# The transposed mixing matrix on the sync queue: half pieces, one a segment, and where its read-back is issued

## The chip, the cores and the metric

The kernel runs on one core of one Trainium2 chip. The metric is device time in microseconds (us), the median of several runs of one program. One further execution is taken by the hardware profiler; the rows in this document are from such profiles.

The engines are named as in the profile: PE is the matrix engine (PEld its weight loads), ACT, DVE and POOL the three elementwise engines, SP the engine that here issues nearly all DMAs. The 16 DMA engines move the data. Each engine works through its own list in order; an instruction waits for the semaphores that it needs, and what stands behind it in the list waits too.

## The reference

A block of attention with a recurrent memory, and then a gated MLP that mixes along the sequence. S = 2048 tokens, width 512, 32 heads of 128, segments of 32 tokens, 8 memory rows, MLP half width 896. Cut to what matters:

```python
mem = mem0
for s in range(64):                                  # part A
    h = concat([mem, ln(x)[32*s:32*s+32]])           # 40 rows
    q, k, v = h @ Wq, h @ Wk, h @ Wv                 # 32 heads
    o = softmax(mask(q @ k.T * scale)) @ v
    o = o @ Wo
    mem, out[s] = o[:8], o[8:]
h = x + concat(out)
z = gelu(ln(h) @ w_in)                               # part B
z1, z2 = z[..., :896], ln(z[..., 896:])
g = w_sp @ z2 + b_sp[:, None]                        # w_sp: 2048 x 2048
h2 = h + (z1 * g) @ w_out
```

The memory rows of a segment come out of the segment before, so the 64 segments of part A run one after the other.

## The kernel before

**Part A** is a loop over `s` (L945 to L1113) that emits one segment after the other. The order in which the code adds operations is the order in which each engine executes them; waits follow from what each operation reads and writes, and from `after=`, a list of operations to wait for. In a segment PE runs, in this order:

- Q and K of 32 rows (L495, 512 columns, four column groups side by side), with the memory rows of the segment before put in by small matmuls (L680);
- scores (L554, L560), the value rows (L495), softmax sums (L575, L496);
- one batch group of matmuls for later segments (L414, L433 or L775);
- probabilities times values (L623, L629), the output projection of eight memory-free rows of earlier segments (L707);
- output sums (`Wo`, L495 and L496 with `f_cT`). They come in two halves by output column: columns 0 to 255 into bank `OB`, evacuated by ACT (`part_evac`, L671), then columns 256 to 511 into `OB2`, evacuated by DVE (L673). The memory rows of the next segment follow from both.

Q, K and V of the last eight rows of each segment don't depend on the memory. They are computed in batches of 16 segments ("batched" rows). The batched V rows go to DRAM (`vext_d`, store L455) and come back segment by segment into one of three buffers `Vx` (`load_vx`, L477), which L629 reads.

**What SP issues for part B beside part A.** The matmul of part B needs `w_sp` transposed. It is read from DRAM in 32 pieces of 64 rows by a transposing DMA into `wst` (L809) and written to DRAM scratch `wT_d` (L810):

```python
def wT_piece(i):
    sp(lambda e: e.dma_start_transpose(out=wst[:, :, :], in_=B_w_sp[i * 64:(i + 1) * 64, :]), writes=["wst"])
    sp(lambda e: e.dma_start(wT_d[i], wst[:, :, :]), reads=["wst"], writes=[("wTd", i)])
```

A piece is issued at the head of each odd segment. There is one buffer `wst`, and the write waits on SP until the transpose has landed. The other DMAs of the loop: `load_h` (L701) and `load_x` (L290) at the head of every fourth segment; the stores of finished rows `h_d` (L728, at the end of segments with s % 4 = 3), `xn_d` (L736, s % 4 = 1), of batch groups (`vext_d` L455, `z2p_d` L786); from segment 36 on the loads of `w_in` (L766) and transposes of `xn_d` (L747). `load_vx(s + 2)` stands near the end of segment s, behind the batch group's store and ahead of the store of `xn_d`.

**Part B** begins in the last segment. `z2_back` (L937) reads rows of z2 from DRAM, `load_wT(0)` (L933) reads the first quarter of the transposed matrix (eight pieces of 256 KB) over the Q weights, behind the last Q matmul (`lastop["q"]`). In the program it stands after the loop, behind four `z2_back` loads and all stores of segment 63, and nine more `z2_back` loads follow. ACT applies the activation to z2 (L1207), DVE normalises it (L1158 to L1169), and PE multiplies it with the transposed matrix (`mix`, L1183), with z1 groups (L1176) between.

Of the kernel before, what the change touches and what calls it, by code (L numbers as in the profile page):

```python
# [169 lines left out]
def fast_path(nc, st, keep, A_x, A_mem0, A_Wq, A_Wk, A_Wv, A_Wo, A_seg_len, B_w_in, B_w_sp, B_b_sp, B_w_out, out):  # L170
# [7 lines left out]
    NSEG = S // SEG  # L178
# [16 lines left out]
    em = Emitter(n_dma_sems=40)  # L195

    def sb(name, shape, dt):
        return st.enter_context(nc.sbuf_tensor("f_" + name, shape, dt))
# [5 lines left out]
    def region(off, n):  # L204
        return arena[:, off:off + n]
# [26 lines left out]
    wst = sb("wst", [128, RB, 64], BF)  # L232
# [25 lines left out]
    wT_d = nc.dram_tensor("wT_d", [S // 64, 128, RB, 64], BF, kind="Internal").ap()  # L258
# [7 lines left out]
    def PB(b):  # L266
        return ("ps", b)

    def sp(fn, **k):
        return em.add("sp", fn, dma=True, **k)  # L270

    def pe(fn, **k):
        return em.add("pe", fn, **k)

    def act(fn, **k):
        return em.add("act", fn, **k)

    def dve(fn, **k):
        return em.add("dve", fn, **k)
# [194 lines left out]
    def load_vx(s):  # L474
        i = s % CK
        assert all(("vext", s // CK, n) in em.last_w for n in range(8))
        sp(lambda e: e.dma_start(Vx[:, s % NVX, :, :], vext_d[s // CK, 8 * i:8 * i + 8, :, :, :].rearrange("t b g e -> g t b e")),  # L477
           reads=[("vext", s // CK, n) for n in range(8)], writes=[("Vx", s % NVX)])
# [14 lines left out]
    def tile_mm(e, out, lhsT, rhs, start, stop, c, held=False):  # L493
        if not held:
            return e.matmul(out, lhsT=lhsT, rhs=rhs, start=start, stop=stop, skip_group_check=True, tile_position=(0, 32 * c))  # L495
        return e.add_instruction(mybir.InstMatmult(  # L496
            name=nc.get_next_instruction_name(), ins=[e.lower_ap(rhs), e.lower_ap(lhsT)], outs=[e.lower_ap(out)],
            start_tensor_calc=start, stop_tensor_calc=stop, tile_size=(128, 32), tile_position=(0, 32 * c),
            bass_skip_group_check=True, ldweights=False))
# [89 lines left out]
    def sm_rcp(b):  # L589
        act(lambda e: e.activation(out=R_sb[:, b, :], in_=R_sb[:, b, :], func=ACT.Exp, scale=-1.0, bias=RBIAS),  # L590
            reads=[("R", b)], writes=[("R", b)])
# [58 lines left out]
    def Wo(cs, bank, d0, d1, bs=(0, 1), first=(0, 0), last=(3, 1), held=None):  # L650
        for c in cs:
            for bg in (4 * b + g for b in bs for g in range(4)):
                b, g = bg // 4, bg % 4
                h = 16 * b + 4 * c + g
                i = 8 * c + bg
                pe(lambda e, h=h, g=g, i=i, b=b, c=c: tile_mm(
                    e, ps[32 * g:32 * g + 32, bank, 0:d1 - d0], cTh[:, i, 8:40], w_o[:, h, d0:d1], (c, b) == first,
                    (c, b) == last, g, (c, b) == held),
                    reads=[("cT", c), ("Wo", b, c)], writes=[PB(bank)])
# [7 lines left out]
    def part_evac(s, half):  # L667
        bank, d0 = (OB, OB2)[half], OC * half
        dst, src = part[:, s % 8, d0:d0 + OC], ps[:, bank, 0:OC]
        if half == 0:  # L670
            act(lambda e: e.activation(out=dst, in_=src, func=ACT.Copy), reads=[PB(bank)], writes=[("part", s % 8, 0)])  # L671
        else:
            dve(lambda e: e.tensor_copy(out=dst, in_=src), reads=[PB(bank)], writes=[("part", s % 8, 1)])  # L673

    def mem_out(s, half):
        bank = GB[half]
        for dc in range(2 * half, 2 * half + 2):
            for c in range(4):
                c0 = dc * 128 + 32 * c
                pe(lambda e, dc=dc, c=c, c0=c0: e.matmul(ps[32 * c:32 * c + 32, bank, dc * M:(dc + 1) * M], lhsT=part[:, s % 8, c0:c0 + 32],  # L680
                                                         rhs=G_sb[:, :], start=True, stop=True, skip_group_check=True, tile_position=(0, 32 * c)),
                   reads=[("part", s % 8, half), "G"], writes=[PB(bank)])
        d2 = slice(2 * half, 2 * half + 2)
        src = ps[:, bank, 2 * half * M:(2 * half + 2) * M].rearrange("p (dc c) -> p dc c", c=M)
        act(lambda e: e.activation(out=hT[:, slot(s + 1), d2, 0:M], in_=src, func=ACT.Copy),  # L685
            reads=[PB(bank)], writes=[("hTm", s + 1, half)])
# [13 lines left out]
    def load_h(rb):  # L700
        sp(lambda e: e.dma_start(hbuf[:, rb % 2, :], xr[:, rb, :]), writes=[("h", rb % 2)])  # L701
# [44 lines left out]
    def xn2T_dma(rb, after):  # L746
        sp(lambda e: e.dma_start_transpose(out=xT2(rb), in_=xn2_d[rb]), reads=[("xn2d", rb)], writes=[("xn2T", rb)],  # L747
           after=after)
# [4 lines left out]
    def xT2(rb):  # L753
        return xts[rb // 4][:, rb % 4, :, :]
# [8 lines left out]
    def load_w_in(half, dc, after):  # L763
        t = (w_in1[:, dc, :], w_in2[dc])[half]
        tok = ("w_in1", "w_in2")[half]
        sp(lambda e: e.dma_start(t, winr[:, dc, half * FH:(half + 1) * FH]), writes=[(tok, dc)], after=after)  # L766
        em.mark_const((tok, dc))
# [37 lines left out]

    NWT = S // 64

    def wT_piece(i):
        sp(lambda e: e.dma_start_transpose(out=wst[:, :, :], in_=B_w_sp[i * 64:(i + 1) * 64, :]), writes=["wst"])  # L809
        sp(lambda e: e.dma_start(wT_d[i], wst[:, :, :]), reads=["wst"], writes=[("wTd", i)])  # L810


    act(lambda e: e.preload_act_table_set("natural_log_exp_and_others"))
# [18 lines left out]
    def start_x(ck, i):  # L832
        start_group(qkx_mm, qkx_evac, ck, i)
# [83 lines left out]
    for ck, n0 in ((2, 2), (3, 0)):  # L917
        for n in range(n0, 8):
# [3 lines left out]
    wTb = [region(0, RB * 512).rearrange("p (t sc c) -> p t sc c", sc=RB, c=64),  # L922
           region(3 * WSZ, RB * 512).rearrange("p (t sc c) -> p t sc c", sc=RB, c=64)]
# [4 lines left out]
    gt = region(2 * WSZ + RB * FH, 2048).bitcast(F32).rearrange("p (j t) -> p j t", j=2)  # L928
    w_out = region(3 * WSZ + RB * 512, FB * D).rearrange("p (fb d) -> p fb d", fb=FB)

    def load_wT(tb, after):
        for t in range(8):
            sp(lambda e, t=t: e.dma_start(wTb[tb % 2][:, t, :, :], wT_d[8 * tb + t]), reads=[("wTd", 8 * tb + t)],  # L933
               writes=[("wT", tb % 2, t)], after=after)

    def z2_back(r0, r1, after):
        sp(lambda e: e.dma_start(z2[:, r0:r1, :], z2p_d[r0:r1].rearrange("r p f -> p r f")),  # L937
           reads=[("z2p", r, hf) for r in range(r0, r1) for hf in range(2)],
           writes=[("z2", r, hf) for r in range(r0, r1) for hf in range(2)], after=[after])

    lastop = {}
# [3 lines left out]
    for s in range(NSEG):  # L945
        j4 = s % 4
        rb = s // 4
        if j4 == 0 and rb > 0:
            load_h(rb - 1)
        if s == NSEG - 1:  # L950
            load_h(rb)
        if s % 2 == 1 and s < NSEG - 1:
            wT_piece(s // 2)
        if s == NSEG - 2:
            wT_piece(NWT - 1)
        if j4 == 0 and 2 <= rb + 2 < RB:
            load_x(rb + 2, 0)
        if s == 4:
# [39 lines left out]
        sm_ln(1)  # L998
        sm_rcp(1)
        if s == NSEG - 1:  # L1000
            xn2T_dma(8, [xops[s]])
            for r in range(4):
                z2_back(r, r + 1, lastop["v"])
        if s + 1 < NSEG:
            qx_copy(s + 1)
# [39 lines left out]
        if s == 0:  # L1045
            start_x(1, 9)
            Wo((0, 2, 1), OB, 0, OC)
            Wo((0, 2, 1), OB2, OC, D)
            Wo((3,), OB, 0, OC)
            part_evac(s, 0)  # L1050
            Wo((3,), OB2, OC, D)
            part_evac(s, 1)
            late += gv.pour(2)
            mem_out(s, 0)
            late += gv.pour(2)
        else:
            Wo((0, 2, 1, 3), OB, 0, OC)
            part_evac(s, 0)
            Wo((3,), OB2, OC, D, (1, 0), (3, 1), (1, 1), (3, 1))
            Wo((0, 2), OB2, OC, D, (0, 1), (3, 1), (1, 1))  # L1060
            if s + 1 < NSEG:
                mem_out(s, 0)
            Wo((1,), OB2, OC, D, (0, 1), (3, 1), (1, 1))
            part_evac(s, 1)
# [22 lines left out]
            late.append(lambda: ring_copy(rb + 2, XB))  # L1087
        for f in late:
            f()
        if s + 2 < NSEG:  # L1090
            load_vx(s + 2)
        if j4 == 1 and rb >= 2:
            xn2_apply(rb - 2, rb % 2)
            xn2_store(rb - 2, rb % 2)
# [7 lines left out]
        if c2 + 8 <= s < c3:  # L1102
            k, m = (s - c2 - 8) // 2, s % 2
# [3 lines left out]
        if s in (c3 + 2, c3 + 4, c3 + 6, c3 + 10, c3 + 14):  # L1107
            r = 9 + (c3 + 2, c3 + 4, c3 + 6, c3 + 10, c3 + 14).index(s)
            xn2T_dma(r, [sops[c3 + 2 * (r - 9) + 1]])
        if s in (c3 + 5, c3 + 7, c3 + 11, c3 + 13):  # L1110
            dc = (c3 + 5, c3 + 7, c3 + 11, c3 + 13).index(s)
            load_w_in(0, dc, [xops[c3 + (3, 6, 10, 13)[dc]]])
    load_wT(0, [lastop["q"]])  # L1113
    for r in range(4, NP):
        z2_back(r, r + 1, lastop["v"])
    sp(lambda e: e.dma_start(bsp_b, bass.AP(B_b_sp.tensor, B_b_sp.offset, [[0, 128], [1, S]])), writes=["bsp"], after=[lastop["k"]])
# [138 lines left out]
    endA = em.by_eng["pe"][-1]  # L1255
    WoX_evac(RB - 1)
    load_wT(1, [endA])
    sp(lambda e: e.dma_start(w_out, B_w_out.rearrange("(fb p) d -> p fb d", p=128)), writes=["w_out"], after=[endA])
    xn2T_pe(RB - 2, 0)
# [755 lines left out]
def build_kernel(nc, A_x, A_mem0, A_Wq, A_Wk, A_Wv, A_Wo, A_seg_len, B_x, B_w_in, B_w_sp, B_b_sp, B_w_out, out):  # L2015
    args = (A_x, A_mem0, A_Wq, A_Wk, A_Wv, A_Wo, A_seg_len, B_w_in, B_w_sp, B_b_sp, B_w_out, out)
    with contextlib.ExitStack() as keep:
        with contextlib.ExitStack() as st:
            em, sems, dsems, flag = fast_path(nc, st, keep, *args)
# [88 lines left out]
```

## Time and profile before

| | us |
|---|---|
| median of three timed runs (854.01 to 854.50) | 854.24 |
| the profiled execution, its own time | 853.86 |
| its span, first to last instruction | 851.7 |
| PE busy in the span | 837.0 |
| DVE, ACT, POOL busy | 538.8, 427.1, 159.8 |

A row of a group gives line, engine, operation, tiles written and read, count, then busy time and mean; in brackets or behind a bar stands the idle time ahead of it and what ended it. "issue" is idle time in which the engine waited for nothing that the profile shows. In the view of stretches, each row is one stretch of time with each engine's busy time and its count of instructions. [...]

### The profile page before, as it was taken

The numbers are of one execution on the slowest core, as the hardware profiler recorded it, in microseconds if no ns is written. First come the engines' busy times: TensorE is split into PE (matmuls) and PEld (weight loads), VectorE is DVE, ScalarE is ACT, GpSimd is POOL, SyncE is SP. The second block draws the span as 40 slices with busy tenths as digits, with TensorE's granted clock in tenths as the row PEclk, the third lists the DMA queues.
The fourth block names the chain that finished last, engine by engine and source line by source line (L and its number), as shares of the span: only waits on it lengthen the run. The fifth ranks groups of instructions, "written<-read, shape, count | busy, mean of one in ns | idle before, by whom it ended". The sixth has DMA issues, their size and how long they took to land.

```text
span 851.7 us, 43893 instructions
## 1 busy us (share of the span) xinstructions
PE 837.0 (98%) x20921; PEld 447.0 (52%) x19133; DVE 538.8 (63%) x1256; ACT 427.1 (50%) x1151; POOL 159.8 (19%) x404
## 2 busy tenths in 40 slices
PE   6999999999999999999999999999999999999997
PEld 5754445555555555556555555555554544444443
DVE  3456677676666666676766666767666676553443
ACT  2455565656555655555655555565656566500000
POOL 5111121122121112121212121211112123200000
PEclk9999999999999999999999999999999999999999
DMA  9972322223212122121323222233322369032001
GB/s 319 379 227 59 75 56 57 54 47 82 57 34 75 34 65 62 26 72 47 64 58 85 55 74 51 81 70 85 91 57 80 96 184 366 2 112 105 33 12 40
DMA packets 105614, 77.21 MB, mean 91 GB/s; under 512 B 63304, under 2 KB 90960, under 8 KB 105424
## 3 DMA queue, kind: packets, MB, share of 16 engines
q1 hardware_dynamic: 105424, 74.35, 30.3%
q8 instruction: 159, 2.61, 1.3%
q14 instruction: 31, 0.25, 0.1%
HBM read 42.38 MB, written 21.59 MB: 75 GB/s over the span
## 4 chain that ended last, share of the span: by engine, by line
PE 95%; DMA 2%; SPq 1%; issue 0%; ACT 0%; DVE 0%; POOL 0%; POOLq 0%
PE f_ps L495 46%; PE f_ps L1183 11%; PE f_ps L496 8%; PE f_ps L414 6%; PE f_ps L707 4%; PE f_ps L1300 3%; PE f_ps L623 3%; PE f_ps L1176 2%; PE f_ps L433 2%; PE f_ps L775 2%; PE f_ps L554 1%; PE f_ps L575 1%; DMA f_arena<-in_A_Wk_dram 1%; PE f_ps L629 1%; PE f_ps L439 1%; PE f_ps L680 1%
## 5 line engine op out<-in xcount | busy, mean ns | idle before, releaser
L495 PE MATMUL f_ps<-f_arena,f_hT 128*32 128x512 bf16 x5120 | 359.5, 380 | 0.3
L495 PEld LDWEIGHTS f_ps<-f_arena,f_hT 128*32 128x32 bf16 x5120 | 117.0, 95 | 153.7 <-issue 63.0
L519 ACT ACTIVATE f_Tst<-f_ps 128x512 bf16<-128x512 f32 (+1 forms) x320 | 150.0, 510 | 77.5 <-PE f_ps L495 77.4
L495 PE MATMUL f_ps<-f_arena,f_cT 128*32 128x256 bf16 x3844 | 127.9, 272 | 0.7 <-ACT f_cT L642 0.5
L495 PEld LDWEIGHTS f_ps<-f_arena,f_cT 128*32 128x32 bf16 x3844 | 94.8, 96 | 27.3 <-ACT f_cT L642 18.2
L615 DVE CAST f_V_sb<-f_ps 128x512 bf16<-128x512 f32 x128 | 88.6, 692 | 25.4 <-PE f_ps L495 25.4
L1183 PE MATMUL f_ps<-f_arena 128*128 128x512 bf16 x448 | 100.9, 379 | 0.6 <-DMA f_arena<-wT_d 0.6
L532 DVE STREAM_TRANSPOSE f_QT<-f_Tst 128x256 uint32<-128x256 uint32 x128 | 57.0, 446 | 68.6 <-ACT f_Tst L519 68.5
L496 PE MATMUL f_ps<-f_arena,f_hT 128*32 128x512 bf16 x1024 | 99.8, 379 | 0.0
L539 POOL COPY f_QT<-f_arena 128x256 bf16<-128x256 bf16 x64 | 30.8, 482 | 313.3 <-PE f_ps L560 313.2
L642 ACT ACTIVATE f_cT<-f_ps 128x320 bf16<-128x320 f32 x128 | 49.0, 435 | 49.1 <-PE f_ps L629 49.1
L644 DVE TENSOR_SCALAR f_cT<-f_ps 128x320 bf16<-128x320 f32 x128 | 56.9, 487 | 25.4 <-PE f_ps L629 25.4
L532 DVE STREAM_TRANSPOSE f_KT<-f_Tst 128x128 uint32<-128x128 uint32 (+1 forms) x192 | 64.5, 349 | 12.9 <-ACT f_Tst L519 12.9
L1183 PEld LDWEIGHTS f_ps<-f_arena 128*128 128x128 bf16 x448 | 43.7, 98 | 53.4 <-DVE f_mv L723 1.0
L673 DVE CAST f_part<-f_ps 128x256 bf16<-128x256 f32 x64 | 27.2, 425 | 67.9 <-PE f_ps L495 67.9
L414 PE MATMUL f_ps<-f_hTe,f_arena 128*128 128x128 bf16 x1024 | 66.9, 223 | 2.2 <-DMA f_arena<-in_A_Wq_dram 1.4
L414 PEld LDWEIGHTS f_ps<-f_hTe,f_arena 128*128 128x128 bf16 x1024 | 59.1, 100 | 7.5 <-ACT f_hTe L395 1.6
L586 ACT ACTIVATE f_R_sb<-f_ps 128x160 f32<-128x160 f32 x128 | 39.1, 305 | 35.9 <-PE f_ps L496 32.7
L1189 DVE TENSOR_TENSOR f_arena<-f_ps,f_arena 128x512 f32<-128x512 f32 x28 | 19.3, 690 | 52.9 <-PE f_ps L1183 52.9
L685 ACT ACTIVATE f_hT<-f_ps 128x16 bf16<-128x16 f32 x126 | 23.3, 185 | 53.4 <-PE f_ps L680 53.0
L671 ACT ACTIVATE f_part<-f_ps 128x256 bf16<-128x256 f32 x64 | 24.6, 385 | 48.4 <-PE f_ps L495 48.4
L544 DVE CAST f_ps<-f_mask 128x224 f32<-128x224 bf16 x128 | 47.1, 368 | 0.0
(118 smaller groups left out, 1094.1 us busy)
## 6 DMA issues: line engine op xcount, KB each, us to landing
wT_d<-f_wst SPq DMA_DIRECT2D x32, 256.0 KB, 2.5
f_arena<-wT_d SPq DMA_DIRECT2D x32, 256.0 KB, 4.8
f_arena<-in_A_Wq_dram SPq DMA_DIRECT2D x4, 1024.0 KB, 8.7
f_arena<-in_A_Wk_dram SPq DMA_DIRECT2D x4, 1024.0 KB, 14.3
f_arena<-in_A_Wv_dram SPq DMA_DIRECT2D x4, 1024.0 KB, 14.5
f_arena<-in_A_Wo_dram SPq DMA_DIRECT2D x8, 512.0 KB, 9.5
f_Vx<-vext_d SPq DMA_DIRECT2D x63, 64.0 KB, 2.9
vext_d<-f_Vs SPq DMA_DIRECT2D x24, 128.0 KB, 2.0
```

The costliest lines, as they stand in the source:

```text
L414: pe(lambda e, h=h, dc=dc, hh=hh: e.matmul(ps[:, bank, hh * 128:(hh + 1) * 128], lhsT=ws[:, dc, h * DH:(h + 1) * DH], rhs=hTe[:, ck % 3, d ...
L495: return e.matmul(out, lhsT=lhsT, rhs=rhs, start=start, stop=stop, skip_group_check=True, tile_position=(0, 32 * c))
L496: return e.add_instruction(mybir.InstMatmult(name=nc.get_next_instruction_name(), ins=[e.lower_ap(rhs), e.lower_ap(lhsT)], outs=[e.lower_a ...
L519: act(lambda e, cs=cs: e.activation(out=Tst[:, tb, cs].rearrange("p (hp i r) -> p hp i r", i=32, r=2), in_=ps[:, bank, cs].rearrange("p (h ...
L532: dve(lambda e, dst=dst, src=src: e.transpose(out=dst, in_=src), reads=tok, writes=wr)
L544: dve(lambda e: e.tensor_copy(out=ps[:, bank, 0:224], in_=mask[:, :]), reads=["mask"], writes=[PB(bank)])
L586: act(lambda e: e.activation(out=R_sb[:, b, :], in_=ps[:, bank, 224:384], func=ACT.Ln, scale=LNS), reads=[PB(bank)], writes=[("R", b)])
L615: dve(lambda e: e.tensor_copy(out=V_sb[:, b, :], in_=ps[:, bank, :]), reads=[PB(bank)], writes=[("V", b)])
L642: act(lambda e: e.activation(out=dst, in_=src, func=ACT.Copy, scale=UNSC), reads=[PB(PVB[c])], writes=[("cT", c)])
L644: dve(lambda e: e.tensor_scalar(out=dst, in0=src, scalar1=UNSC, scalar2=None, op0=ALU.mult), reads=[PB(PVB[c])], writes=[("cT", c)])
L707: pe(lambda e, h=h, g=g, i=8 * qr + bg: e.matmul(ps[32 * g:32 * g + 32, WXB, :], lhsT=cTx[:, rb % 2, i, :], rhs=w_o[:, h, :], start=(i < 4 ...
L1183: pe(lambda e: e.matmul(ps[:, bank, 0:TB], lhsT=z2[:, sc, fb * 128:(fb + 1) * 128], rhs=wTb[tb % 2][:, :, sc, :], start=(n == 0), stop=(n ...
```

## The change

`w_sp` is transposed in 64 half pieces (64 rows by 1024 columns), which alternate between the two halves of `wst`. At the head of each segment from 1 on one half is issued (two in segments 6 and 10), and then the write of the half before it, then `load_vx(s + 1)` (which stood as `load_vx(s + 2)` at the end of the segment before). The transpose waits for `lastop["wa"]`: the last matmul of the first half of the output sums (bank `OB`) of the segment before. `load_h`, `load_x` and `load_xe` come behind these. `load_wT(0)` moves into segment 63, behind the last Q: four pieces, then the transpose of `xn_d` and two `z2_back`, then four pieces, then two `z2_back`.

```diff
-    def wT_piece(i):
-        sp(lambda e: e.dma_start_transpose(out=wst[:, :, :], in_=B_w_sp[i * 64:(i + 1) * 64, :]), writes=["wst"])
-        sp(lambda e: e.dma_start(wT_d[i], wst[:, :, :]), reads=["wst"], writes=[("wTd", i)])
+    def wT_in(p, after):
+        i, k = p // 2, p % 2
+        sp(lambda e: e.dma_start_transpose(out=wst[:, 8 * k:8 * k + 8, :], in_=B_w_sp[i * 64:(i + 1) * 64, 1024 * k:1024 * k + 1024]),
+           writes=[("wst", k)], after=after)
+
+    def wT_out(p):
+        i, k = p // 2, p % 2
+        sp(lambda e: e.dma_start(wT_d[i][:, 8 * k:8 * k + 8, :], wst[:, 8 * k:8 * k + 8, :]), reads=[("wst", k)],
+           writes=[("wTd", i, k)])
+
+    wp = [0]
+
+    def wT_step(s):
+        for _ in range(2 if s in (6, 10) else 1):
+            p = wp[0]
+            if p < 2 * NWT:
+                wT_in(p, [lastop["wa"]])
+            if 0 < p <= 2 * NWT:
+                wT_out(p - 1)
+            wp[0] += 1
...
-    def load_wT(tb, after):
-        for t in range(8):
+    def load_wT(tb, after, ts=range(8)):
+        for t in ts:
...
     for s in range(NSEG):
         j4 = s % 4
         rb = s // 4
+        if s > 0:
+            wT_step(s)
+        if 0 < s < NSEG - 1:
+            load_vx(s + 1)
         if j4 == 0 and rb > 0:
             load_h(rb - 1)
         if s == NSEG - 1:
             load_h(rb)
-        if s % 2 == 1 and s < NSEG - 1:
-            wT_piece(s // 2)
-        if s == NSEG - 2:
-            wT_piece(NWT - 1)
...
         if s == NSEG - 1:
+            load_wT(0, [lastop["q"]], range(4))
             xn2T_dma(8, [xops[s]])
-            for r in range(4):
+            for r in range(2):
+                z2_back(r, r + 1, lastop["v"])
+            load_wT(0, [], range(4, 8))
+            for r in range(2, 4):
                 z2_back(r, r + 1, lastop["v"])
...
             Wo((0, 2, 1, 3), OB, 0, OC)
+            lastop["wa"] = em.by_eng["pe"][-1]
             part_evac(s, 0)
...
-        if s + 2 < NSEG:
-            load_vx(s + 2)
...
-    load_wT(0, [lastop["q"]])
     for r in range(4, NP):
```

More of the change, by code (lines that the diff above doesn't have):

```diff
@@ L929, in fast_path @@
     w_out = region(3 * WSZ + RB * 512, FB * D).rearrange("p (fb d) -> p fb d", fb=FB)
-    def load_wT(tb, after):
-        for t in range(8):
-            sp(lambda e, t=t: e.dma_start(wTb[tb % 2][:, t, :, :], wT_d[8 * tb + t]), reads=[("wTd", 8 * tb + t)],
+    def load_wT(tb, after, ts=range(8)):
+        for t in ts:
+            sp(lambda e, t=t: e.dma_start(wTb[tb % 2][:, t, :, :], wT_d[8 * tb + t]), reads=[("wTd", 8 * tb + t, 0), ("wTd", 8 * tb + t, 1)],
                writes=[("wT", tb % 2, t)], after=after)
@@ L1057, in fast_path @@
             Wo((0, 2, 1, 3), OB, 0, OC)
+            lastop["wa"] = em.by_eng["pe"][-1]
             part_evac(s, 0)
```

## The prediction

> **What bounds the kernel now.** I read the page's head and its chain first.
>
> ```profile
> span 851.7 us, 43893 instructions
> PE 837.0 (98%) x20921; PEld 447.0 (52%) x19133; DVE 538.8 (63%) x1256; ACT 427.1 (50%) x1151; POOL 159.8 (19%) x404
> PE 95%; DMA 2%; SPq 1%; issue 0%; ACT 0%; DVE 0%; POOL 0%; POOLq 0%
> ```
>
> PE sets the time. The change neither adds nor takes a PE instruction, so it can only win time in which PE stands, or make it stand. The view of waits on PE names one wait that the change touches (0.6 us, for the transposed matrix at the start of part B); nothing else after the start-up is over 0.5 us. But waits without a name are easily missed there, so I laid stretches over the loop. The bounds are starts of ACT's evacuation at L671, once a segment.
>
> ```profile
> L671 ACT ACTIVATE f_part<-f_ps x64: 384/385/386, 53.1 to 692.3; 128x256 bf16<-128x256 f32 x64
> ```
>
> ```profile
> core 0: us, PE busy (x), PEclk, DMA share, GB/s
> 73.30:123.71 50.41, 50.34 (x1549) 1.00 0.28 68
> 347.14:397.73 50.59, 50.59 (x1542) 1.00 0.24 59
> 591.25:641.72 50.47, 50.47 (x1562) 1.00 0.28 69
> 326.26:336.38 10.12, 10.12 (x315) 1.00 0.40 94
> 336.38:347.14 10.76, 10.43 (x316) 1.00 0.12 35
> 418.07:428.78 10.71, 10.49 (x316) 1.00 0.61 102
> 449.07:459.58 10.51, 10.39 (x314) 1.00 0.31 90
> ```
>
> The first three rows are five calm segments each: 10.08, 10.12 and 10.09 us a segment. The last three rows are single segments that take 0.64, 0.59 and 0.39 to 0.42 us more with the same work (x314 to x316) at the same clock (1.00). In all, 63 segments take 692.3 - 53.1 = 639.2 us; at the calm pace (8 at 10.08 up to 134 us, 34 at 10.12 up to 479 us, 21 at 10.09) they would take 636.6. So **2.6 us are lost in stops inside segments**, 1.6 of them in three. Two of the stops in the order of time on PE, and SP ahead of them:
>
> ```profile
> 337.10 0.39 PE L433 MATMUL f_ps<-f_arena,f_hTe 128*32 128x512 bf16 x3
> 337.81 0.38 PE L433 MATMUL f_ps<-f_arena,f_hTe 128*32 128x512 bf16 x1 [0.33 <-issue]
> ...
> 426.43 0.39 PE L707 MATMUL f_ps<-f_arena,f_cTx 128*32 128x512 bf16 x2
> 427.04 0.40 PE L707 MATMUL f_ps<-f_arena,f_cTx 128*32 128x512 bf16 x4 [0.22 <-issue]
> ```
>
> ```profile
> 332.78 1.33 SPq L809 DMA_TRANSPOSE f_wst<-in_B_w_sp_dram  x1
> ...
> 421.92 1.27 SPq L809 DMA_TRANSPOSE f_wst<-in_B_w_sp_dram  x1
> ```
>
> PE stops in the midst of a group of four equal matmuls, with nothing to wait for, 4.3 and 4.5 us after a transpose of `w_sp` was issued. What is late is PE's own program, as the queues show (whole span; then the stretches 333.7 to 335.3 and 335.2 to 336.4):
>
> ```profile
> q8 instruction: 159, 2.61, 1.3%
> ...
> q1 hardware_dynamic: 841, 0.21, 79.5%
> ...
> q1 hardware_dynamic: 513, 0.12, 50.4%
> q8 instruction: 1, 0.02, 5.8%
> ```
>
> ```profile
> 337.70:427.00 89.30, 89.02 (x2675) 50.38 (x2427) 61.23 (x151) 52.22 (x149) 18.65 (x45) 1.00 0.24 55
> 333.65:336.99 3.34, 3.34 (x131) 2.60 (x128) 2.11 (x6) 1.42 (x4) 0.78 (x3) 1.00 0.59 107
> ```
>
> 159 packets of 2.61 MB / 159 = 16.4 KB, against 20921 + 19133 PE instructions: one packet for some 252. Between the two stops lie 2675 + 2427 = 5102 instructions, 20.2 packets: they stand on packet borders. The packet for the first stop's border isn't among the 841 small ones that fill 79.5% of the DMA engines until 335.3; it comes at 335.3, in their tail, and PE runs dry at 337.1. The last row shows why there: that packet's worth of PE work (131 + 128 instructions) takes 3.34 us, where the mean is 89.30 / 20 = 4.5. Scores, sums and values are short instructions, the 512-column Q and K matmuls long ones. **A stop needs a crowded DMA moment while PE is in short instructions.**
>
> **The change part by part.**
>
> *Half pieces.* A full piece:
>
> ```profile
> L809 SPq DMA_TRANSPOSE f_wst<-in_B_w_sp_dram x32: 1247/1334/2727, 58.2 to 676.4; - x32
> DMA to landing us min/median/max: 3.2/4.3/5.6
> ```
>
> The crowd lasts from about 334.1 (issue 332.78 + 1.33) to about 335.9 (half of 335.2 to 336.4 busy): 1.8 us. A half moves half the packets: I estimate 0.9 us (bounds 0.9, half, and 1.8, if the duration is fixed). SP issues 32 more transposes of 1.33 us and 32 more writes; with a Vx load of 0.56 it is 2.2 us a segment of 10.1, and SP has no other use for the time.
>
> *Their place.* The wait is for the first half of the output sums, which is what L671 waits for, so issue comes at the bounds of the stretches above. Data starts 1.3 us later and ends by 2.3, while PE does the second half of the sums and then Q and K, where a packet lasts longest. That is the calm place, unless SP arrives late: stores ahead in its list hold it. Such a row is
>
> ```profile
> 451.06 0.32 SPq L728 DMA_DIRECT2D h_d<-f_hbuf  x1
> ```
>
> 2.0 us after 449.07. In a late segment, with the bound (L671) ahead,
>
> ```profile
> 672.15 0.39 ACT L671 ACTIVATE f_part<-f_ps 128x256 bf16<-128x256 f32 x1 [0.87 <-PE f_ps L495]
> ```
>
> ```profile
> 675.25 0.60 SPq L736 DMA_DIRECT2D xn_d<-f_xo  x1
> 675.89 0.44 SPq L766 DMA_DIRECT2D f_arena<-in_B_w_in_dram  x1
> ```
>
> it is 675.89 + 0.44 - 672.15 = 4.2 us. Then a half's data runs 5.5 to 6.4 us after the bound (4.2 + 1.3), into the scores of the next segment.
>
> Laying halves at those places over PE's packet borders, I find one or two small stops. I take: both `w_sp` stops go (1.2), of the remaining 1.4 a half goes (some had transposes of `w_sp` near, some only other loads; the 449.07 segment had two loads of `w_in` and two of x and none of `w_sp`), so **-1.9 us**. Bounds: -2.6 (no stop left), 0 (they only move), and above nothing in the last rival.
>
> *What waits behind the new wait.* The write of the half before, `load_vx`, `load_h`, `load_x`, and the stores of the segment. The write's own wait is done a segment earlier, save in segments 6 and 10, where SP stands 4.3 + 2.5 us for piece and write. A Vx row now issued at most some 7 us after the bound lands 2.9 us later and is used 1.5 segments (15 us) after: cost 0; without that cover L629 would stand. x is needed by DVE at the segment's end, 10 us on; h a segment later: 0. A store of a batch group stands ahead of the next wait: 0. PE gets no new signal, since L671 waits for the same matmul already.
>
> *load_wT(0).* The rows of before:
>
> ```profile
> 685.19 1.19 SPq L747 DMA_TRANSPOSE f_arena<-xn_d  x1
> 689.07 1.75 SPq L937 DMA_DIRECT2D f_arena<-z2p_d  x4
> ...
> 694.55 3.77 SPq L933 DMA_DIRECT2D f_arena<-wT_d  x8
> ```
>
> ```profile
> 703.62 0.59 PE L1183 MATMUL f_ps<-f_arena 128*128 128x512 bf16 x2 [0.56 <-DMA f_arena<-wT_d]
> ```
>
> ```profile
> 686.12 0.60 ACT L519 ACTIVATE f_Tst<-f_ps 128x512 bf16<-128x512 f32 x1 [0.21 <-PE f_ps L495]
> ...
> 693.96 0.95 ACT L1207 ACTIVATE f_arena<-f_arena 128x896 bf16<-128x896 bf16 x1
> ```
>
> The last Q ends at 686.1. Four loads at 3.77 / 8 = 0.47 give 688.0, the transpose 689.2, and the first z2 row is issued at 689.2 in place of 689.07. The last four loads then go out at 690.1 to 692.0 in place of 694.55 to 698.3, some 6 us sooner, so the wait of **0.56 us goes**. What is late next: the z2 row for L1207 at 693.96. In the quiet stretch of before it took
>
> ```profile
> f_arena<-z2p_d SPq DMA_DIRECT2D x4, 224.0 KB, 2.7
> ```
>
> and with 1 MB ahead of it perhaps 2 us more: 689.2 + 4.7 = 693.9, just in time. Later z2 loads come about 4 us sooner. I take -0.56, bounds -0.6 and +1 (ACT late by one such delay).
>
> **The sum**, against the profiled execution's own 853.86: 853.86 - 1.9 - 0.56 = 851.4. The median of the timed runs is 0.38 above that execution, so I forecast **851.8**.
>
> [...]
>
> **The rivals.**
>
> 1. *The stops aren't the program's late packets, or cannot be moved by making transposes shorter.* Then only the wait at part B goes: 854.24 - 0.56 = 853.7. For it: the third stop had no transpose. Against it: both large stops stand on packet borders behind a transpose, and the calm pace is exact elsewhere. [...] Chance 0.22.
>
> 2. *Stops change place and grow in number: slower.* There are 62 crowded moments in place of 32, and where SP is held by stores they fall into the scores and values, where a packet lasts 3.34 us. The price of one is 10.76 - 10.12 = 0.64. With the old 2.6 and 0.56 gone it decides from 5 stops on (3.2 us); to be over 0.2% slower it takes 8 (3.2 + 1.7 = 4.9). If a half's crowd lasts as long as a full one's and every fifth falls badly, 12 stops: 854.24 - 3.2 + 7.7 = 858.7. Against it: full pieces without any fixed place made two such stops in 32. Chance 0.12.
>
> 3. *All stops go*: 854.24 - 2.6 - 0.56 = 851.1. Against it: the `w_in` loads and the transposes of `xn_d` stay. Chance 0.16.
>
> **How the numbers follow.** Forecast (851.1 to 852.8) 0.50, rival 3 0.16, rival 1 0.22, rival 2 0.12. 0.2% is 1.7 us, about what a measurement of this kernel can tell from no change. Under 852.5 lie rival 3 and most of the forecast's case: faster 0.62. Rival 1, the rest of the forecast and a mild rival 2: same 0.27. The rest, slower 0.11. For 8 in 10 the range takes rivals 3 and 1: 850.8 to 854.3, the lower end 0.3 under rival 3, since the timed runs may lose more in stops than the profiled one.
>
> **What would show it.** Right: at the bounds of L671 no segment over 10.3 us; no PE row with idle time put down to "issue" in the loop; landing of a half well under 4.3 us; the 703.62 row without its wait. Wrong: single segments still over 10.5 us with a transpose of `w_sp` issued about 4 us ahead of the stop (rival 2), or the same three stops (rival 1); PE waiting at L629 for Vx, or ACT at L1207 for z2 (a cover that I took for granted).

## The result and the profile after

| | before | after |
|---|---|---|
| median of 22 timed runs each, same chip, us | 854.46 | 852.89 |
| lowest and highest run, us | 853.29, 856.65 | 851.62, 854.23 |
| the profiled execution, its own time, us | 853.86 | 853.28 |

The ratio is 0.9978, 95% interval 0.9971 to 0.9984: 1.6 us faster by the medians, 1.9 by the ratio (1.4 to 2.5). The forecast was 851.8 against 854.24, 2.4 us. Direction and range held; the sum was too large, and the timed runs below show in which term.

The page's head and the queues of the profile after:

```profile
span 851.0 us, 43989 instructions
PE 837.0 (98%) x20921; PEld 447.1 (53%) x19133; DVE 538.9 (63%) x1256; ACT 426.7 (50%) x1151; POOL 159.2 (19%) x404
...
q8 instruction: 159, 2.61, 1.3%
...
wT_d<-f_wst SPq DMA_DIRECT2D x64, 128.0 KB, 2.5
```

PE's work is the same to the instruction, and its program still comes in 159 packets (q8; 2.61 MB / 159 = 16.4 KB each). The half transposes (the line of the transpose; L810 in the kernel after):

```profile
L810 SPq DMA_TRANSPOSE f_wst<-in_B_w_sp_dram x64: 1200/1231/3000, 56.7 to 676.0; - x64
DMA to landing us min/median/max: 2.6/3.3/5.3
```

Issue still takes 1.23 us where a full piece took 1.33; landing comes at 3.3 in place of 4.3. So the data part did shrink by about 1 us, near the 0.9 estimated.

**Part B.** SP, PE and ACT in order of time, after:

```profile
686.60 1.74 SPq L950 DMA_DIRECT2D f_arena<-wT_d  x4
688.39 1.19 SPq L747 DMA_TRANSPOSE f_arena<-xn_d  x1
689.63 1.62 SPq L954 DMA_DIRECT2D f_arena<-z2p_d  x2
691.29 1.86 SPq L950 DMA_DIRECT2D f_arena<-wT_d  x4
```

```profile
701.85 1.69 PE L1164 MATMUL f_ps<-f_arena 128*128 128x448 bf16 x8
703.38 1.03 PE L1203 MATMUL f_ps<-f_arena 128*128 128x512 bf16 x4
```

```profile
694.45 0.95 ACT L1227 ACTIVATE f_arena<-f_arena 128x896 bf16<-128x896 bf16 x1
```

The first mixing matmul (L1203, L1183 before) starts 1.53 us after the z2 group ahead of it, with no wait in the row; before it was 703.62 - 701.36 = 2.26 (the group's start at 701.36 is from the trace of before). That is 0.73 us, and every later PE row keeps it to the end.

**The loop.** Here the two profiles differ in place, not in sum:

```profile
L671 ACT ACTIVATE f_part<-f_ps x64: 384/384/385, 53.4 to 692.8; 128x256 bf16<-128x256 f32 x64
```

692.8 - 53.4 = 639.4 us for 63 segments, where before had 639.2. The stretches, with the same bounds as before (starts of L671; the first row is five segments):

```profile
core 0: us, PE busy (x), PEclk, DMA share, GB/s
347.82:398.43 50.61, 50.61 (x1543) 1.00 0.23 55
337.54:347.82 10.28, 10.28 (x315) 1.00 0.15 37
418.82:429.02 10.20, 10.20 (x314) 1.00 0.35 95
439.13:449.93 10.80, 10.30 (x327) 1.00 0.13 33
296.68:307.19 10.51, 10.46 (x314) 1.00 0.18 47
```

The calm pace is the same (10.12). The two large stops of before are nearly gone (10.76 became 10.28, 10.71 became 10.20). But a segment that was calm before now takes 10.80, and another 10.51. In all, eight segments of this profile are over 10.25 us, where before had five: more stops, most of them smaller. One execution is one draw of the stops: in 22 runs before spreads over 3.4 us. The sum of stops of one profile can't be set against that of another; timed runs must do it.

### The profile page after: what moved, and what is told of

The parts are those of the page before. It is cut to its first block, busy times and chain, and to the rows that moved or that the text cites. A ratio compares the mean times of both kernels' runs of the same rounds, so it can differ in the third digit from the quotient of the medians.

```text
span 851.0 us, 43989 instructions
## 1 busy us (share of the span) xinstructions
PE 837.0 (98%) x20921; PEld 447.1 (53%) x19133; DVE 538.9 (63%) x1256; ACT 426.7 (50%) x1151; POOL 159.2 (19%) x404
## 3 DMA queue, kind: packets, MB, share of 16 engines
q8 instruction: 159, 2.61, 1.3%
## 4 chain that ended last, share of the span: by engine, by line
PE 96%; DMA 1%; SPq 1%; issue 0%; ACT 0%; POOL 0%; DVE 0%; POOLq 0%
PE f_ps L495 46%; PE f_ps L1203 11%; PE f_ps L496 8%; PE f_ps L414 6%; PE f_ps L707 4%; PE f_ps L1320 3%; PE f_ps L1196 3%; PE f_ps L623 3%; PE f_ps L433 2%; PE f_ps L775 2%; PE f_ps L554 1%; PE f_ps L575 1%; DMA f_arena<-in_A_Wk_dram 1%; PE f_ps L629 1%; PE f_ps L439 1%; PE f_ps L680 1%
## 5 line engine op out<-in xcount | busy, mean ns | idle before, releaser
L1203 PE MATMUL f_ps<-f_arena 128*128 128x512 bf16 x448 | 100.9, 379 | 0.0
L1203 PEld LDWEIGHTS f_ps<-f_arena 128*128 128x128 bf16 x448 | 43.7, 98 | 52.6
L671 ACT ACTIVATE f_part<-f_ps 128x256 bf16<-128x256 f32 x64 | 24.6, 384 | 47.5 <-PE f_ps L495 47.5
```

The costliest lines, as they stand in the source:

```text
L1203: pe(lambda e: e.matmul(ps[:, bank, 0:TB], lhsT=z2[:, sc, fb * 128:(fb + 1) * 128], rhs=wTb[tb % 2][:, :, sc, :], start=(n == 0), stop=(n ...
```

## The experiments

Each was timed against the kernel before on its chip; the medians of before on the five chips were 854.3 to 855.5, so ratios are compared, not times.

Theory 1: PE stops where a packet of its program comes late, and transposes of `w_sp` make packets late; the gain has a part in the loop and a part at the start of part B. Rivals are named at each run.

| kernel | median, us | before, us | ratio | 95% interval |
|---|---|---|---|---|
| tail_only | 854.24 | 855.07 | 0.9991 | 0.9982 to 1.0001 |
| halves_only | 853.45 | 855.07 | 0.9982 | 0.9969 to 0.9996 |
| no_wsp | 852.43 | 855.07 | 0.9970 | 0.9960 to 0.9981 |
| halves_scores | 854.48 | 855.07 | 0.9997 | 0.9988 to 1.0007 |
| change_again | 852.76 | 854.25 | 0.9984 | 0.9975 to 0.9993 |
| full_fixed | 853.42 | 854.25 | 0.9992 | 0.9983 to 1.0001 |
| halves_free | 853.63 | 854.25 | 0.9987 | 0.9976 to 0.9997 |
| doubled | 854.60 | 854.25 | 1.0007 | 0.9997 to 1.0017 |
| shifted | 852.60 | 855.46 | 0.9968 | 0.9957 to 0.9980 |
| late_direct | 852.37 | 855.46 | 0.9964 | 0.9952 to 0.9976 |
| late_spread | 851.81 | 855.46 | 0.9957 | 0.9944 to 0.9970 |
| late_shift64 | 851.89 | 855.35 | 0.9957 | 0.9943 to 0.9971 |

### The two parts alone

tail_only, on the kernel before:

```diff
         if s == NSEG - 1:
+            load_wT(0, [lastop["q"]], range(4))
             xn2T_dma(8, [xops[s]])
-            for r in range(4):
+            for r in range(2):
+                z2_back(r, r + 1, lastop["v"])
+            load_wT(0, [], range(4, 8))
+            for r in range(2, 4):
                 z2_back(r, r + 1, lastop["v"])
...
-    load_wT(0, [lastop["q"]])
```

> The kernel before with only the loads of the first quarter of the transposed matrix moved into the last segment. Theory 1 (the gain has two parts: the wait ahead of the first mixing matmul, 0.6 to 0.7 us, and shorter stops in the loop, about 0.9): 0.6 to 0.7 us faster than before, 0.9992. Rival (the loop gives nothing, stops only change place): 1.3 to 1.6 us faster, as much as the whole change, 0.9983.

halves_only, on the kernel after, is the same diff the other way round.

> The change without the move of the loads of the first quarter: half pieces at the head of each segment alone. Theory 1: 0.7 to 1.0 us faster than before, 0.999, and the wait of about 0.6 us ahead of the first mixing matmul is still there. Rival (the loop gives nothing): within 0.2 us of before.

Measured: 0.9991 (0.8 us, interval -0.1 to 1.5) and 0.9982 (1.5 us, interval 0.3 to 2.6). The first is what the two traces say of part B (0.73), though its interval alone would also admit no gain, and its rival's 1.3. The second is more than the 0.7 to 1.0 expected, with an interval that holds both; the wait of 0.6 us at part B is still in its trace, as expected. The loop alone is faster with its whole interval below 1, so the rival that the loop gives nothing falls. Whole minus tail gives the loop 1.9 - 0.8 = 1.1 us (and 1.4 - 0.8 = 0.6 by change_again, below); halves_only alone says more. Between 0.6 and 1.5 the runs don't decide.

### How much the transposes cost at all

no_wsp, on the kernel before:

```diff
-        if s % 2 == 1 and s < NSEG - 1:
-            wT_piece(s // 2)
-        if s == NSEG - 2:
-            wT_piece(NWT - 1)
...
     def load_wT(tb, after):
...
-            wT_d[8 * tb + t]
+            B_w_sp[64 * (8 * tb + t):64 * (8 * tb + t) + 64, :].rearrange(...)
```

> The kernel before without any transpose of w_sp or write of it in the loop; the loads of part B take the same bytes of w_sp untransposed, so the mixing is computed with another matrix. Theory 1 (transposes of w_sp cause more than half of the stops in the loop): 1.3 to 2 us faster than before, excess over the calm pace in the loop under 1.2 us, where before has 2.4. Rival (the stops have other causes): excess as before, 2.2 to 2.6 us, time within 0.3 us of before.

Measured: 0.9970, 2.6 us (1.6 to 3.4), more than the 1.3 to 2 expected. The seven runs lie between 852.0 and 853.2 where before's 31 on this chip lie between 852.3 and 857.9. But not all of it is the loop: in the trace of no_wsp the wait ahead of the first mixing matmul is gone too, which is 0.65 us from the matmul ahead of it, start to start. That leaves some 1.9 us for the transposes in the loop. So they cause much of the time lost there in a typical execution, and probably much of its spread. The one profile shows less of it than expected: its loop takes 638.2 us against 639.2 before, 1.6 over the calm pace where under 1.2 was expected. Stops remain; stretches of no_wsp:

```profile
417.04:427.92 10.88, 10.49 (x317) 1.00 0.25 71
438.03:448.14 10.11, 10.11 (x325) 1.00 0.02 3
```

The first still loses 0.76 us, with no transpose in the whole loop but those of `xn_d`, which begin some 40 us later; two loads of `w_in` stand there.

### Place and length

halves_scores, on the kernel after:

```diff
-        if s > 0:
-            wT_step(s)
...
         lastop["s"] = sops[s] = em.by_eng["pe"][-1]
+        if s > 0:
+            wT_step(s)
...
-                wT_in(p, [lastop["wa"]])
+                wT_in(p, [lastop["s"]])
```

> The change with each half piece issued behind the last score matmul of the segment, so that its data moves while PE is in sums, values and output sums, its short instructions. Theory 1 (a stop needs a crowded moment while PE is in short instructions): more stops than the change, at least 6 of 0.3 to 0.6 us, 2 to 4 us slower than the change. Rival (the place of the transposes doesn't matter): within 0.3 us of the change.

Measured: 0.9997, against 0.9978 and 0.9984 of the change: 1.1 to 1.6 us slower, less than the 2 to 4 expected, but the loop's gain is gone. So the place matters by the times (the interval lies above the change's first one and overlaps with change_again's). That it does so through more stops is not shown: I expected six more of 0.3 to 0.6 us, and the one profile, its fastest run, has seven segments over 10.25 us where the change has eight and, in its second profile, four.

The next four ran on one chip. change_again is the changed kernel, unedited.

> The changed kernel itself, as the measure for the three kernels beside it on this chip, and for a second profile of its stops: both theories expect 0.9978 within its interval, and an excess in the loop that is not the same as in its first profile, at mostly the same segments.

full_fixed, on the kernel after, replaces the half pieces:

```diff
+    def wT_in(i, after):
+        sp(lambda e: e.dma_start_transpose(out=wst[:, :, :], in_=B_w_sp[i * 64:(i + 1) * 64, :]), writes=["wst"], after=after)
...
+    def wT_step(s):
+        if s % 2 == 0 or s == NSEG - 1:
+            wT_out((s - 1) // 2 if s < NSEG - 1 else NWT - 1)
+        if (s % 2 == 1 and s < NSEG - 1) or s == NSEG - 2:
+            wT_in(s // 2 if s < NSEG - 2 else NWT - 1, [lastop["wa"]])
```

> The change with full pieces: one at the head of each odd segment behind the first half of the output sums, its write at the head of the next. Theory 1 (place and length both count; in the calm place a full piece still ends before PE is in short instructions): within 0.5 us of the change. Rival (the gain in the loop comes from the half size, since SP arrives late in many segments and a full crowd then runs into the scores): 0.7 to 1 us slower than the change, nothing left of the loop's gain.

halves_free, on the kernel after:

```diff
-                wT_in(p, [lastop["wa"]])
+                wT_in(p, [])
```

> The change without the wait for the first half of the output sums: half pieces, one a segment, issued as soon as SP gets to them. Theory 1 (the place counts): 0.5 to 0.9 us slower than the change, near the kernel before with only the loads of the first quarter moved. Rival (the size alone counts): within 0.3 us of the change.

doubled, on the kernel after:

```diff
     def wT_in(p, after):
...
+        if s >= 14:
+            sp(lambda e: e.dma_start_transpose(out=xn[:, 1, :].rearrange("p (a b) -> p a b", b=64),
+                                               in_=B_w_sp[i * 64:(i + 1) * 64, 1024 * k:1024 * k + 1024]), writes=[("xn", 1)])
```

> The change with each half piece from segment 14 on read and transposed a second time right behind, into a spare buffer: twice the crowd from the same place. Theory 1: the second half's data ends some 4 us behind the bound and, where SP is late, in the scores: 0.5 to 1.5 us slower than the change, not more. Rival (any transposing traffic costs PE time wherever it stands, by bytes): 64 halves cost about what taking the transposes of w_sp out of the kernel before won, 2 us or more.

Measured: change_again 0.9984; full_fixed 0.9992 (0.7 us slower by the ratios, what its rival said); halves_free 0.9987 (0.3 us by the ratios, 0.9 by the medians); doubled 1.0007 (1.8 to 2.0 us slower, over theory 1's 1.5 and about at its rival's 2). The intervals of change_again, full_fixed and halves_free overlap, so length and place are not told apart by them: each looks worth some tenths. doubled is clear: 49 more halves cost 1.8, 0.037 each, and no_wsp won some 1.9 in the loop for 32 full pieces with their writes, 0.03 a half. But doubled doesn't price the place of the change, since the second half of each pair is issued behind the first, 4.2 us behind the bound in the median.

And the change itself seldom reaches its place. SP in a segment of the profile after whose bound (the start of L671) is 429.02:

```profile
431.65 0.35 SPq L736 DMA_DIRECT2D xn_d<-f_xo  x1
432.05 1.79 SPq L810 DMA_TRANSPOSE f_wst<-in_B_w_sp_dram  x1
```

SP stood at the store of `xn_d` and issued the half 3.0 us behind the bound. Over that whole profile 18 of the 64 halves are issued within 0.5 us of the bound and 40 more than 2 us behind it; the median is 2.4 us. In halves_free, without the wait, it is 3.0, in before 3.6, in halves_scores 6.2. So halves_free hardly moves the halves, and what the change's place gains against halves_scores is a dear place avoided. full_fixed comes nearest to the bound, with 16 of its 32 pieces within 0.5 us and a median of 0.7, and is not faster. Whether a half right behind the output sums is free was not tested by itself.

change_again also gave a second profile:

```profile
417.58:428.27 10.69, 10.48 (x317) 1.00 0.33 90
438.39:449.18 10.79, 10.29 (x327) 1.00 0.13 33
```

The stop near 439 us is there again with the same size (0.68 over 10.11), at the same matmul. In the first profile after, PE and SP in order of time, and the packet's worth of work ahead of the stop:

```profile
439.85 0.39 PE L379 MATMUL f_ps<-f_ident,f_xn 128*32 128x128 bf16 x13
440.73 0.24 PE L379 MATMUL f_ps<-f_ident,f_xn 128*32 128x128 bf16 x3 [0.49 <-issue]
```

```profile
434.51 0.56 SPq L477 DMA_DIRECT2D f_Vx<-vext_d  x1
439.13 1.22 SPq L810 DMA_TRANSPOSE f_wst<-in_B_w_sp_dram  x1
```

```profile
436.91:439.90 2.99, 2.99 (x129) 2.35 (x128) 1.76 (x5) 1.19 (x4) 0.40 (x1) 1.00 0.03 5
```

Nothing was issued for 4.6 us ahead of 439.13, and the DMA engines were nearly idle (share 0.03). The packet, 129 + 128 instructions, took 2.99 us. **A stop can come without a crowd, behind a short packet.** But a short packet is not enough for one. Three rows: the same segment in before, the same matmuls in no_wsp (16 in one row, with no idle time), and the shortest packet of the loop in the profile after:

```profile
438.90:449.07 10.17, 10.17 (x328) 1.00 0.01 4
```

```profile
438.75 0.40 PE L379 MATMUL f_ps<-f_ident,f_xn 128*32 128x128 bf16 x16
```

```profile
233.62:236.60 2.98, 2.98 (x130) 2.33 (x128) 1.78 (x5) 1.17 (x4) 0.40 (x1) 1.00 0.02 5
```

There is no stop in any of them (10.17 in before is 0.06 over the calm 10.11). What differs in these traces is when the next packet's transfer began. From 437 to 441 us the profile after has one,

```profile
q8 instruction: 1, 0.02, 2.2%
```

by its record from 438.14 to 439.52: it began 1.2 us behind the start of the packet that PE was in, and PE went on at 440.73, 1.2 us behind its end. In no_wsp the same transfer began 0.6 us behind, at the packet of 2.98 us 0.4 us. Why it begins now sooner and now later is open.

### Are they packet borders?

shifted, on the kernel after:

```diff
     late_consts()
+    for i in range(64):
+        pe(lambda e, i=i: e.matmul(ps[0:32, 5, i:i + 1], lhsT=ident[:, 0:32], rhs=ident[:, i:i + 1], start=True, stop=True),
+           reads=["ident"], writes=[PB(5)])
     xT(0, 6)
```

> The change with 64 matmuls of one column (128 PE instructions, half a program packet) ahead of the first transposes, while PE waits for the first rows anyway; their results aren't used. Theory 1 (stops stand on borders of PE's program packets, where the packet holds short instructions): within 0.7 us of the change, but the stops move to other segments: the one of 0.68 us near 438 us, the same in several profiles, is under 0.2, and new ones stand near some of 115, 216, 317, 388, 490, 520, 560 and 652 us, where the shortest packets then end. Rival (they belong to what those segments load or compute): the stops near 418 and 438 us stay, 0.4 to 0.7 us each.

Stretches of its profile:

```profile
418.29:428.40 10.11, 10.11 (x314) 1.00 0.36 94
438.52:448.64 10.12, 10.12 (x326) 1.00 0.14 36
114.27:124.56 10.29, 10.25 (x327) 1.00 0.18 49
316.87:327.24 10.37, 10.37 (x327) 1.00 0.14 35
489.71:500.21 10.50, 10.24 (x313) 1.00 0.34 85
458.75:469.51 10.76, 10.22 (x306) 1.00 0.31 59
```

The segments near 418 and 438 us are calm, though they compute and load what they did. (One calm profile proves little alone: 418 is nearly calm in the profile after, 438 in before.) Three of the eight named places have a stop of 0.2 to 0.4 us here (115, 317, 490), a fourth (520) one of 0.2, the others under 0.1; and 459 us has one of 0.64 that I had not named. The first stretch of the loop, 10.07 us in before, takes 10.60.

A count over all 14 profiles decides it. I numbered PE's instructions of each trace in order of start: matmuls, weight loads and the 170-odd others. Behind 50 us there are 40 PE rows with over 0.1 us of idle time put down to "issue". With the 159 packets of the profile after, (20921 + 19133 + 171) / 159 = 253 instructions come to a packet. Divided by 256, the numbers of the 40 all leave a remainder of 190 to 195, in shifted too, where 128 more instructions stand ahead. At all 40, PE went on 1.2 to 1.7 us behind the end of an instruction packet's transfer, and at no packet border between 45 and 690 us sooner than 1.2. So the stops stand on packet borders, and PE waits there for its program. The rival falls. The time, 0.9968, is 0.9 to 1.4 us better than the change's by the ratios, where at most 0.7 was expected; the intervals overlap.

### A version that beats both

late_direct, on the kernel after: 16 halves in the loop, the rest into part B's buffers. Its `load_wT_direct(1)` stands behind the loads of `h_sb`.

```diff
-        for _ in range(2 if s in (6, 10) else 1):
+        for _ in range(1):
             p = wp[0]
-            if p < 2 * NWT:
+            if p < 16:
                 wT_in(p, [lastop["wa"]])
-            if 0 < p <= 2 * NWT:
+            if 0 < p <= 16:
...
+    def load_wT_direct(tb, after):
+        for t in range(8):
+            i = 8 * tb + t
+            sp(lambda e, t=t, i=i: e.dma_start_transpose(out=wTb[tb % 2][:, t, :, :], in_=B_w_sp[i * 64:(i + 1) * 64, :]),
+               writes=[("wT", tb % 2, t)], after=after)
...
-    load_wT(1, [endA])
...
+    load_wT_direct(1, [endA])
...
-            load_wT(tb + 2, [])
+            load_wT_direct(tb + 2, [])
```

> The change with only the first quarter of w_sp in half pieces in the loop (segments 1 to 16); the other three quarters are transposed straight into the buffers of part B, where PE's packets last some 27 us, in place of being written to DRAM and read back. Theory 1: about three quarters of what the transposes still cost in the loop goes, 1.0 to 1.5 us faster than the change, 0.997 of before. Rival (what is left in the loop has other causes, or part B now waits for a transpose): within 0.4 us of the change, or slower with a wait at the mixing matmuls.

late_spread, on late_direct (the four loads at the end of segments 36 and 39 leave):

```diff
+        if s in (37, 38, 39, 40):
+            dc = (0, 2, 1, 3)[s - 37]
+            o = 35 if dc in (0, 2) else 38
+            load_w_in(1, dc, [(xops, sops)[dc // 2][o], lastop["wa"]])
```

> As late_direct, and the four loads of the second half of w_in go out one a segment in segments 37 to 40, behind the first half of the output sums, in place of two and two at the end of segments 36 and 39. Theory 1: the stop near 418 us (0.5 to 0.9) goes, 0.3 to 0.7 us faster than late_direct. Rival (that packet is short enough to be late without any load): within 0.2 us of late_direct, stop still there.

late_shift64, on late_spread, has the loop of shifted with `range(32)`.

> late_spread with 32 matmuls of one column (64 PE instructions, a quarter of a program packet) ahead of the first transposes, their results unused. Counted out on a trace of the loop, the shortest packet then takes 3.28 us in place of 3.05. Theory 1: another 0.3 to 1 us faster, 0.995 of before; the stops near 438 and 540 us go. Rival (the borders' place is worth nothing on the whole, other packets come short): within 0.3 us of late_spread, 0.9957.

Measured: late_direct 0.9964 (3.1 us faster than before), late_spread 0.9957 (3.7 us). Beyond the change's 0.9978 to 0.9984 that is 1.2 to 1.7 and 1.8 to 2.3 us; the step from late_direct to late_spread, 0.6 us, was expected at 0.3 to 0.7, but the two intervals overlap. late_spread's interval lies below both of the change's; late_direct's overlaps with them a little, and wholly with that of shifted, which left every transpose in the loop. PE waits for no transpose in part B of late_direct. Three stretches of late_spread, near 418, 438 and 479 us, and then the one near 418 us in late_direct:

```profile
417.77:427.88 10.11, 10.11 (x314) 1.00 0.17 47
438.00:448.53 10.53, 10.30 (x326) 1.00 0.09 25
478.77:489.35 10.58, 10.38 (x325) 1.00 0.01 3
```

```profile
417.22:427.34 10.12, 10.12 (x315) 1.00 0.25 70
```

The segment near 418 us is calm in late_spread, but it is so in late_direct too, with the loads of `w_in` where they were. So it is not shown that spreading them took the stop away. The stops near 438 and 479 us come with the DMA engines nearly idle; they don't always come (10.17 near 438 in before, 10.09 near 479 in late_direct). late_shift64 took the one at 438 away, yet gave it back at once, in its second segment:

```profile
52.93:64.14 11.21, 10.41 (x301) 1.00 0.24 66
438.82:448.93 10.11, 10.11 (x326) 1.00 0.10 28
```

The first stretch takes 1.14 us more than the 10.07 it takes in late_spread. On the whole it is late_spread's 0.9957, as its rival said; the interval leaves room for 1.2 us either way.

## Why the prediction was right in sign and too large

- **The bound, and the stops as late program packets: held.** All 40 stops counted stand at nearly the same remainder by 256 instructions, and PE goes on 1.2 to 1.7 us behind the end of a packet's transfer.
- **"A stop needs a crowded DMA moment while PE is in short instructions": failed.** 2.99 us of work with DMA share 0.03 ended in a stop, so no crowd is needed; 2.98 us with share 0.02 did not, so a short packet doesn't decide it either. At 36 of the 40 stops the transfer began over 1.1 us behind the border ahead, which it does at a quarter of all borders. That transposes add to the loss is shown by no_wsp and doubled.
- **"-1.9 us" in the loop: mis-sized.** The runs give 0.6 to 1.1 by difference, 1.5 by halves_only (interval 0.3 to 2.6). Two things went into it. I let both `w_sp` stops of one profiled execution stand for the typical one and took both as gone, and I counted on issue at the bound, which 18 of 64 halves reach. Taking every transpose out wins some 1.9 in the loop, as much as the term; halving and moving them wins a third to four fifths of that.
- **The signs: mixed.** The landing (3.3 us) and the row without its wait came as named for "right". But five segments are over 10.3 us, and a PE row has idle time put down to "issue" (at 440.73). For the two over 10.5 us no transpose of `w_sp` was issued about 4 us ahead of the stop, as rival 2's sign has it.
- **"-0.56 us" at part B: right in mechanism, 0.73 in size.** The idle time in a row is counted from the end that the row ahead gives, 701.36 + 1.69 = 703.05 before; in the profile after the mixing matmul starts 0.16 us ahead of that end (703.38 against 701.85 + 1.69), so start to start the wait was longer. Tail_only gave 0.8.
- **The z2 row "just in time": ACT did not wait for it.** L1227 starts right at the end of the table load, 1.7 us behind L671, as before (693.96 - 692.3 = 1.7).
- **Rival 1** (only part B gains) falls by halves_only. That the stops weren't the program's late packets falls by the 40 stops counted; and a packet of 3 us in a quiet stretch (DMA share 0.03) ran PE dry, and the packet that PE stood for began its transfer only 1.2 us behind the border ahead. **Rival 2** (stops change place and grow in number) came in its mechanism in the first profile, eight segments over 10.25 us for five (four in the second), but not in its price: the new stops are mostly small, and the time fell. **Rival 3** (all stops go) falls by the profile after.

## What to carry to other kernels

When the bounding engine is busy to 98% and still loses time that no wait explains, lay equal stretches over a loop and look for one that is longer with the same count of instructions; then count instructions between the stops, and see whether they fit the size of a program packet (here 16.4 KB, some 253 PE instructions). DMA scheduling took only part of such stops away here; moving transfers to a stage whose packets last long (part B, where 64 mixing matmuls with their weight loads, half a packet, take 13.81 us in the profile after) did better by the ratios (late_direct 0.9964, late_spread 0.9957) than halving and placing them (0.9978 and 0.9984), and moving the borders (shifted, 0.9968) came near it. One profile is one draw: where stops come and go by execution, size a gain from the spread of timed runs, not from the stops of one trace.

## What the runs showed of the hardware that was not expected

- PE can run dry with DMA engines nearly idle (share 0.03): behind a packet whose work took 2.99 us, with the stop 440.73 - 436.91 = 3.8 us from border to border. The same packet in no_wsp took 3.1 us without a stop; there the next transfer began 0.6 us behind the border, here 1.2. In the 14 profiles the transfer of an instruction packet took 0.9 to 2.2 us, and between 45 and 690 us PE never began the packet sooner than 1.2 us behind the transfer's end.
- 128 PE instructions of no use at the start, 0.3% of the program, went with stops in other segments in the profile of shifted: near 438 us 10.12 us in place of 10.80, near 459 us 10.76 in place of 10.06.
- A transpose of half the size costs SP nearly the same to issue: 1.23 us against 1.33.

Left open: how much of the loop's gain is length and how much place (the intervals of full_fixed and halves_free overlap with the change's), what a half costs where it is issued right behind the output sums, and why a packet's transfer begins 0.6 us behind a border in one execution and 1.2 in another.
